# RWKV attention and a 16-expert layer on one core: two early experts split in two items, first steps reordered, one PSUM pool

## The chip, the cores and the metric

The kernel runs on one core of a Trainium2 chip. The metric is the device time of one execution in microseconds (us). The engines are called by the names of the profile: PE (TensorE matmul), PEld (its weight loads), DVE (VectorE), ACT (ScalarE), POOL (GpSimd) and SP (SyncE, which here only issues DMAs). PSUM is the memory that matmuls write[...].

## What is computed

An attention block with a decaying state, whose rows then go through a mixture of experts in two levels. Everything is f32. B, H, S, D are 4, 8, 768, 48; the 3072 rows have 384 columns; there are 4 groups of 4 experts, 1024 hidden columns each.

```python
for t in range(S):
    kt, vt, rt = (k[:, :, t], v[:, :, t], r[:, :, t])
    cur = np.einsum('bhd,bhe->bhde', u[None] * kt, vt)
    y[:, :, t] = np.einsum('bhd,bhde->bhe', rt, state + cur)
    state = w[None, :, :, None] * state + np.einsum('bhd,bhe->bhde', kt, vt)
...
x = attn_out.transpose(0, 2, 1, 3).reshape(B * S, H * D)
g_idx = np.argmax(x @ w_group, axis=1)
e_idx = np.argmax(xg @ w_expert[g], axis=1)
h = np.maximum(xg[mask_e] @ w1[g, e], 0.0)
ye = h @ w2[g, e]
out[tok_idx] = (g_w * e_w)[:, None] * ye
```

Each row goes to one expert only; `g_w` and `e_w` are the softmax weights of the chosen group and the chosen expert.

## The kernel before

**The token loop.** The 3072 rows are 24 tiles of 128 (`NT`). Step s of the loop at L714 handles tile s: 128 tokens of one batch entry, the four entries in turn, so four steps are one chunk of tokens, and a group of k, r and v loads (`load`, L284) holds two tiles. Inside a tile the recurrence is written as matmuls. k is scaled by powers of the inverse decay (`iw`) and r by powers of the decay (`pw`). `turn` (L435) transposes k or r of a tile on PE, and `turn_out` copies the result out of PSUM: k by ACT into `kT`, r by DVE, times `pw`, into `rT`. `scores` (L460) multiplies them into `PA`; `mask` (L478, DVE) copies the upper triangle into `am`, whose diagonal (the u term) was written before by `diagonal_here` (DVE) and `diagonal` (ACT, one instruction for each head). The diagonal comes from `own` (POOL: r times k times u, two products of 1.0 us) and `sum_own` (DVE). `values` (L509) multiplies `am` with v into the lower half of the two banks of `YB`; `state` (L497) adds what the earlier chunks left, and `update` and `carry` (L518, L529) renew that state R. `values_out` copies the result to `yT` on ACT. `scaled` (L425, POOL) makes the scaled k.

**Routing.** `rows_out` (L555) transposes `yT` back into rows, `gate_parts` and `gate_sum` make the 20 gate logits, and `route_1` to `route_5` choose the expert of each row, count places (`route_prefix`, on PE, with running sums `cum`), and scatter rows by indirect DMAs of POOL into `x_sorted` in device memory, one region of 3200 rows for each expert. After 12 tiles, in step 14, `choose_two` picks the two fullest experts; their weights are loaded in pieces (`early_piece`, 8 pieces of 384 KB for each expert) from step 16 on. After the last tile, `choose_rest` orders the other 14 by their counts, and `judge` decides whether a slow second pass is needed (L949); it is not run with these inputs.

**The expert stage** (L833 on) has 16 items, one for each expert, in the order of `SLOTS` (224 rows down to 164). For an item, `fetch_rows` loads rows, `columns` transposes them on DVE in blocks of 32 into `xe`, `up` runs 24 matmuls into `hT` (ReLU on ACT), `arrange` reorders w2 on ACT, `down` runs 24 matmuls whose result is still transposed, `finish` transposes it back on DVE, multiplies by the gate and scatters it in blocks of 32 rows by 4 quarters (6 or 7 indirect DMAs). Weights have two buffers: `fetch_weights(s + 2)` is issued behind the first `down` of item s.

**What sets the order.** The order on every engine is the order in which the code issues (`manual_schedule`, L76); semaphores come from the tiles' dependencies. SP, POOL, ACT, DVE and PE each work through their own queue in order. The loop has its own PSUM pool with six tiles (`PA`, `YB`: two banks each; `TR`, `RW`, `MS`, `SB`: one each); the expert stage opens another pool with four banks for `ph` and four for `po`. Ahead of the loop (L687 to L711) the first two tiles are prepared: `iw` is transposed into `RW`, k of tile 0 is scaled on DVE by it (`scaled_here`), and then turned.

Of the kernel before, what the change touches and what calls it, by code (L numbers as in the profile page):

```python
# [19 lines left out]
SLOTS = [224, 216, 212, 208, 208, 202, 202, 200, 200, 196, 194, 188, 186, 174, 172, 164]  # L20
# [7 lines left out]
def kernel(  # L28
# [78 lines left out]
    two_f = cst([P, 2], "two_f")  # L107
    two_i = cst([P, 2], "two_i", I32)
    cnt_s = cst([P, GE], "cnt_s")
# [112 lines left out]

    with ExitStack() as rec:
        ring = rec.enter_context(tc.tile_pool(name="ring", bufs=1))
        pool = rec.enter_context(tc.tile_pool(name="wkv", bufs=2))
        psum = rec.enter_context(tc.tile_pool(name="psum", bufs=1, space=bass.MemoryType.PSUM))

        def ps(shape, name):
            return psum.tile(shape, FP32, name=name)

        PA = ps([P, 2, 512], "PA")
        YB = ps([P, 2, 512], "YB")
        TR = ps([P, HC, P], "TR")
        RW = ps([P, NQ, P], "RW")
        MS = ps([P, 512], "MS")
        SB = ps([P, 512], "SB")
        y_ps = YB[:, :, 0 : 2 * P]
        RT = YB[:, :, 2 * P : 4 * P].rearrange("p b (h t) -> p b h t", t=P)
        lT_ps = TR[:, 0, :]
# [18 lines left out]
        SQ = spare([P, HC, 8])  # L258
        RK = spare([P, HC, 8])
        held_at = spare_at[0]  # L260
        SPARE = (held_at, held_at + 4 * NL, held_at + 4 * NL + 4 * GE)
# [36 lines left out]
        raw[0, "k"], raw[0, "r"] = place(0, "kt", 3), place(0, "rt", 3)  # L298
        for a in range(2):
            load_half(raw[0, "k"], k, 0, a, both[a])  # L300
            load_half(raw[0, "r"], r, 0, a, both[1 - a])
            if a == 0:
                nc.scalar.dma_start(
                    out=ub.rearrange("p h d -> p (h d)"),
                    in_=bass.AP(tensor=u.tensor, offset=u.offset, ap=[[0, P], [1, H * D]]),
                )
        zeros = ring.tile([P, XW], FP32, name="zeros")
# [4 lines left out]
        raw[0, "v"] = load(v, 0, "vt", 4)  # L312
        raw[1, "r"] = load(r, 1, "rt", 3)
        raw[1, "k"] = load(k, 1, "kt", 3)
# [3 lines left out]

        pw = ring.tile([P, HC, P], FP32, name="pw")
# [3 lines left out]
        make_identity(nc, ident)  # L323
        nc.gpsimd.memset(gwp, 0.0)
# [4 lines left out]
        for t in am[0:2]:  # L329
            nc.gpsimd.memset(t[:, 0], 0.0)  # L330
        nc.gpsimd.tensor_add(sel, ident[:, 0:NL], ident[:, 32 : 32 + NL])
        for q in range(2, NQ):
            nc.gpsimd.tensor_add(sel, sel, ident[:, 32 * q : 32 * q + NL])
# [499 lines left out]
    with ExitStack() as moe:  # L833
# [90 lines left out]
        for job in left:  # L924
            job()
# [294 lines left out]
```

## Time and profile before

| | us |
|---|---|
| median of 3 runs (lowest, highest) | 431.27 (428.61, 431.41) |
| the profiled execution, its own time | 432.07 |
| its span, first to last instruction | 430.3 |
| PE busy | 382.4 (89%) |
| POOL busy | 208.3 (48%) |
| ACT busy | 192.2 (45%) |
| DVE busy | 151.4 (35%) |
| moved by DMA | 82.02 MB, 191 GB/s |
| first `values` | 14.14 |
| last work of the loop on PE begins | 141.64 |
| first matmul of the expert stage | 159.77 |
| last copy out of PSUM begins | 417.75 |

The profile is that of one execution; all times in the text are counted from the start of its span. The clock of PE is the share of full speed that was granted (0.960 in the mean). Matmuls are pipelined and their ends are modelled, so what a series of them costs is read from start to start. An f32 matmul appears as two instructions, a transpose as one. A wait for several semaphores is put down to the one that came last.

### The profile page before, as it was taken

How to read it: one execution, taken by the hardware profiler on the slowest of the kernel's cores; microseconds unless marked ns; L12 is line 12 of the kernel's file. 1: busy time of each engine (PE TensorE's matmuls, PEld its weight loads, DVE VectorE, ACT ScalarE, POOL GpSimd, SP SyncE). 2: the span in 40 equal slices, each digit the busy share in tenths (PEclk: the TensorE clock that was granted, in tenths of full speed). 3: DMA queues.
4: the chain of work that ended last, by engine and by line, in shares of the span. 5: the costliest groups of instructions: out<-in, count | busy, mean ns of one | idle time of the engine just before them, and what ended most of it. 6: DMA issues, size and time to landing. Idle time of an engine off the chain costs nothing.

```text
span 430.3 us, 10330 instructions
## 1 busy us (share of the span) xinstructions
PE 382.4 (89%) x3874; PEld 366.1 (85%) x3874; DVE 151.4 (35%) x389; ACT 192.2 (45%) x461; POOL 208.3 (48%) x270
## 2 busy tenths in 40 slices
PE   2777999999798429999999999999999999999980
PEld 2556899988787319999999999999999999999970
DVE  6735788788666521102022022022022022022110
ACT  3668788887575122333424423423423424433410
POOL 7669939796812530062362452542542543352435
PEclk9999999999999858999999999999999999999995
DMA  9799989956969263979799889889899899999000
GB/s 146 111 168 172 205 179 205 201 112 149 218 187 272 105 175 54 248 175 268 169 236 270 184 224 263 206 238 246 216 245 243 219 248 261 220 269 247 23 23 27
DMA packets 122905, 82.02 MB, mean 191 GB/s; under 512 B 96420, under 2 KB 114020, under 8 KB 122848
## 3 DMA queue, kind: packets, MB, share of 16 engines
q1 hardware_dynamic: 114976, 70.98, 72.6%
q0 software_dynamic: 4960, 9.55, 7.8%
q10 hardware_dynamic: 2912, 0.77, 1.0%
q8 instruction: 32, 0.52, 0.6%
q14 instruction: 25, 0.20, 0.2%
HBM read 70.09 MB, written 11.68 MB: 190 GB/s over the span
## 4 chain that ended last, share of the span: by engine, by line
issue 44%; PE 24%; POOL 17%; DMA 6%; DVE 4%; ACT 3%; POOLq 1%; DVEq 0%; ACTq 0%
POOL out_dram L916 16%; PE PA L472 5%; PE YB L513 5%; DMA out_dram<-yt,idn 5%; PE TR L442 3%; ACT am L491 2%; PE YB L504 2%; PE YB L442 2%; PE RW L558 2%; PE TR L548 2%; PE MS L524 1%; DVE am L479 1%; PE MS L572 1%; POOL x_sorted L215 1%; DMA x_sorted<-xt,place_i 1%
## 5 line engine op out<-in xcount | busy, mean ns | idle before, releaser
L916 POOL DMA_INDIRECT out_dram<-yt,idn x107 | 104.0, 972 | 166.6 <-DVE yt L914 124.6
L892 PE MATMUL ph<-xe,w 128*128 128x200 f32 (+12 forms) x768 | 132.6, 333 | 7.9 <-DMA w<-in_moe_w_dram 7.9
L892 PEld LDWEIGHTS ph<-xe,w 128*128 128x128 f32 x768 | 129.8, 192 | 8.4 <-ACT w2p L882 8.0
L904 PE MATMUL po<-hT,w2p 128*128 128x200 f32 (+12 forms) x768 | 130.4, 330 | 0.0
L904 PEld LDWEIGHTS po<-hT,w2p 128*128 128x128 f32 x768 | 128.1, 190 | 0.0
L913 DVE STREAM_TRANSPOSE yt<-yT 128x672 f32<-128x672 f32 (+1 forms) x16 | 13.6, 847 | 209.8 <-ACT yT L907 209.8
L897 ACT ACTIVATE hT<-ph 128x416 f32<-128x416 f32 (+12 forms) x64 | 31.9, 498 | 101.1 <-PE ph L892 101.1
L491 ACT ACTIVATE am<-ident,du 128x128 f32<-128x128 f32 x184 | 60.5, 397 | 6.1 <-DVE du L431 6.0
L882 ACT COPY w2p<-w 128x1024 f32<-128x1024 f32 x48 | 47.0, 1046 | 11.9 <-POOL yT L839 11.9
L907 ACT COPY yT<-po 128x208 f32<-128x208 f32 (+12 forms) x48 | 15.5, 322 | 69.2 <-PE po L904 67.3
L215 POOL DMA_INDIRECT x_sorted<-xt,place_i x24 | 24.0, 998 | 36.5 <-ACT lT L553 27.4
L479 DVE COPY_PREDICATED am<-later,PA 128x1024 f32<-128x1024 int32 x24 | 31.5, 1313 | 6.7 <-PE PA L472 6.6
L513 PE MATMUL YB<-am,vt 128*48 128x128 f32 x384 | 27.0, 282 | 5.2 <-DVE am L479 2.6
L513 PEld LDWEIGHTS YB<-am,vt 128*48 128x48 f32 x384 | 20.5, 125 | 10.2 <-issue 4.9
L422 POOL TENSOR_TENSOR dg<-rp,kt 128x384 f32<-128x384 f32 x24 | 24.2, 1009 | 6.7 <-DMA rp<-in_r_dram 4.7
L472 PE MATMUL PA<-rT,kT 48*64 48x128 f32 (+1 forms) x736 | 25.8, 258 | 0.0
L423 POOL TENSOR_TENSOR dg<-dg,ub 128x384 f32<-128x384 f32 x24 | 24.2, 1007 | 2.0 <-DMA ub<-in_u_dram 0.2
L472 PEld LDWEIGHTS PA<-rT,kT 48*64 48x64 f32 x736 | 20.1, 134 | 4.3 <-issue 4.0
L426 POOL TENSOR_TENSOR kp<-kt,T 128x384 f32<-128x384 f32 x22 | 22.3, 1012 | 2.7 <-DMA kt<-in_k_dram 2.7
L542 ACT COPY yT<-YB 128x512 f32<-128x512 f32 x24 | 14.0, 582 | 17.2 <-PE YB L513 17.2
L455 DVE TENSOR_TENSOR rT<-YB,pw 128x512 f32<-128x512 f32 x22 | 15.2, 691 | 17.4 <-PE YB L442 14.6
L451 ACT COPY kT<-TR 128x512 f32<-128x512 f32 x24 | 14.0, 585 | 11.8 <-PE TR L442 11.8
(137 smaller groups left out, 313.9 us busy)
## 6 DMA issues: line engine op xcount, KB each, us to landing
w<-in_moe_w_dram SPq DMA_DIRECT2D x128, 384.0 KB, 9.4
vt<-in_v_dram SPq DMA_DIRECT2D x24, 192.0 KB, 5.1
kt<-in_k_dram SPq DMA_DIRECT2D x23, 192.0 KB, 4.2
rp<-in_r_dram SPq DMA_DIRECT2D x23, 192.0 KB, 5.8
xg<-x_sorted SPq DMA_DIRECT2D x42, 85.8 KB, 3.9
out_dram<-yt,idn POOLq DMA_INDIRECT x107
x_sorted<-zeros SPq DMA_DIRECT2D x4, 392.0 KB, 6.1
xg<-x_sorted SPq DMA_DIRECT2D x20, 73.5 KB, 5.3
```

What stands on the lines that cost most here:

```text
L215: ins = nc.gpsimd.indirect_dma_start(out=xs_dram, out_offset=bass.IndirectOffsetOnAxis(ap=place_i[:, i : i + 1], axis=0), in_=xt[:, i].rea ...
L422: nc.gpsimd.tensor_mul(dg, raw[g, "r"][:, a], raw[g, "k"][:, a])
L423: nc.gpsimd.tensor_mul(dg, dg, ub)
L472: nc.tensor.matmul(PA[64 * z : 64 * (z + 1), e, P * hc + 64 * z : P * (hc + 1)], lhsT=kT[rows, hc, 64 * z : 64 * (z + 1)], rhs=rT[rows, hc ...
L479: nc.vector.copy_predicated(am[n % NAM], later.unsqueeze(1).unsqueeze(1).to_broadcast([P, 2, HC, P]).bitcast(I32), PA.rearrange("p e (h t) ...
L491: nc.scalar.mul(am[n % NAM][:, e, hc, :], ident, du[:, e, hc : hc + 1])
L513: nc.tensor.matmul(y_at(e, hc), lhsT=vt[:, n % 2, 2 * hc + e, :], rhs=amn[:, e, hc, :], start=(n < 4 and hc < 2), stop=True, skip_group_ch ...
L882: nc.scalar.copy(o4[:, kk], v4[:, kk])
L892: nc.tensor.matmul(ph[:, i, 0:n], lhsT=w1[:, ko, P * (f + i) : P * (f + i + 1)], rhs=xe[:, ko].rearrange("p i b -> p (i b)")[:, 0:n], star ...
L897: nc.scalar.activation(hTs[s][:, f : f + 2, 0:n], ph[:, :, 0:n], AF.Relu)
L904: nc.tensor.matmul(po[:, 0:n], lhsT=w2p[:, d, fo, :], rhs=hT[:, fo, 0:n], start=(fo == 0), stop=(fo == FO - 1))
L916: ins = nc.gpsimd.indirect_dma_start(out=out_q, out_offset=bass.IndirectOffsetOnAxis(ap=idn[:, i : i + 1].bitcast(U32), axis=0), in_=yt[:, ...
```

## The change

1. *Two items for each early expert.* The first 128 rows (`AHEAD`) of each of the two early experts are loaded in step 21 (`rows_ahead`), transposed in step 23, and run through both projections right behind the loop (`up_ahead`, `down_ahead`), between the parts of the last routing. Their rest (96 and 88 rows) are items of the expert stage: one first, one last. The second projection of all four uses `hT` as the stationary operand and w2 as the moving one (`rows_down`), so its result has whole rows and goes out in one indirect DMA.
2. *The choice* is moved: the keys are made in step 14 and the choice in step 15; k, r and v that would be loaded in step 16 are issued ahead of it. A count over 16 tiles in step 22 (`bases`) tells how many rows of the two experts were taken ahead.
3. *The expert stage* has three weight buffers that rotate, besides that of the expert held for the last item; weights are fetched for item p + 3. `ph` takes four banks in turn and `po` two, out of one PSUM pool that serves the loop too.
4. *The first steps.* k and r of tile 0 are turned unscaled and multiplied by `iw` and `pw` on DVE; in steps 0 to 5 (`CLOSE`) the scores of the next tile and the rows of the last stand in front of the turns, and the gate logits of the first tiles are put off to steps 3 to 7. u comes as one row that a matmul spreads. Five of eight diagonals of a first tile are written by DVE, the others by ACT. Loads of groups 1 and 2 are issued ahead of the gate weights. Small constants are made in other steps.
5. *Banks.* The turned r goes to `RW`, the rows of `rows_out` to the upper half of `YB`, and the gates use `MS` and `TR` in turn at first.

The diff, cut to its core:

```diff
-SLOTS = [224, 216, 212, 208, 208, 202, 202, 200, 200, 196, 194, 188, 186, 174, 172, 164]
+AHEAD = 128
+SLOTS = [96, 88, 212, 208, 208, 202, 202, 200, 200, 196, 194, 188, 186, 174, 172, 164]
...
+    def rows_down(hT, w2, i, n, po, yt):
+        for fo in range(FO):
+            nc.tensor.matmul(
+                po[0:n, 0:DM], lhsT=hT[:, fo, 0:n], rhs=w2[:, fo, :], start=(fo == 0), stop=(fo == FO - 1),
+                skip_group_check=True,
+            )
+        nc.scalar.mul(yt[0:n], po[0:n, 0:DM], tagA[i][0:n, 1:2])
+        ins = nc.gpsimd.indirect_dma_start(
+            out=out, out_offset=bass.IndirectOffsetOnAxis(ap=idA[i][0:n].bitcast(U32), axis=0),
+            in_=yt[0:n], in_offset=None, bounds_check=N - 1, oob_is_err=False,
+        )
...
-        for hc in range(HC):
-            nc.tensor.transpose(RW[:, hc, :], iw[:, hc], ident)
-        turn(0, "rT", MS.rearrange("p (h t) -> p h t", t=P), early=True)
-        scaled_here(0, 0)
-        own(0, 0)
-        turn(0, "kT")
-        turn_out(0, "rT")
+        turn(0, "rT", MS.rearrange("p (h t) -> p h t", t=P))
+        turn_first()
+        for hc in range(HC):
+            nc.tensor.transpose(rows_ps[:, hc // 2, P * (hc % 2) : P * (hc % 2 + 1)], iw[:, hc], ident)
+        nc.scalar.copy(
+            T2.rearrange("p (b y) d -> p b y d", b=2),
+            rows_ps.rearrange("p b (y x) -> p b y x", x=DP)[:, :, :, 0:D],
+        )
+        own(0, 0)
+        scaled(0, 1)
+        own(0, 1)
+        scaled(0, 0)
...
+            if s == NT - 9:
+                loads(g + 1)
+            if s == NT - 3:
+                rows_ahead(0)
+                rows_ahead(1)
...
             values(s)
-            update(s)
             values_out(s)
+            if s == 0:
+                own_term(1)
+            for n, e, hc in waiting:
+                diagonal(n, e, hc, hc + 1)
+            if s <= CLOSE:
+                scores(s + 1)
+                update(s)
+                if s == CLOSE:
+                    sum_own(s + 3)
+                mask(s + 1)
             carry(s)
-            far = s + (3 if s > 2 else 2)
+            far = s + (2 if s < CLOSE else 3)
+            if 1 <= s < CLOSE:
+                rows_out(s - 1)
             if far < NT:
                 turn(far, "kT")
+                turn(far, "rT")
...
         c = NB - 1
+        out_0 = up_ahead(0, 0, PA[:, 0, 0:256])
         gate_sum(NT - 1)
         rows_out(NT - 1)
+        out_0()
         route_1(c)
         route_e(c)
         route_2(c)
-        route_p(c)
+        up_ahead(0, 2, YB[:, 0, 0:256])()
+        up_ahead(0, 4, TR.rearrange("p q t -> p (q t)"), partial(route_p, c))()
         route_3(c)
         route_4(c)
         route_5(c, range(4))
         choose_rest()
-        judge(same)
+        judge()
+        for i in range(2):
+            tokens(i, AHEAD, base_f[:, i : i + 1])
+        up_ahead(1, 0, PA[:, 0])()
+        down_ahead(0, YB[:, 0])
+        up_ahead(1, 4, RW.rearrange("p q t -> p (q t)"))()
+        down_ahead(1, TR.rearrange("p q t -> p (q t)"))
...
         fetch_rows(0)
-        for job in left:
-            job()
         fetch_rows(1)
-        arrange(0)
+        fetch_weights(1)
+        fetch_rows(2)
+        fetch_weights(2)
         columns(0)
...
+            if order[p] < 2:
+                rows_down(hTs[p], held(p)[1], 2 + i, SLOTS[i], po, yt)
+            else:
+                down(p, 0)
+            if p + 3 < last:
+                fetch_weights(p + 3)
```

`up_ahead(i, f, bank)` runs the matmuls of `up` for 128 columns, two or four column groups at a time, and gives back the ReLU as a call; `order` is experts 1 to 15 and then 0; `rows_ahead(i)` is four DMAs of rows and one of row numbers and gates.

## The prediction

> **What bounds the kernel now.** I read four views in this order: the page's 40 slices, the windows around the end of the token loop, the timeline of TensorE at the start, and the timeline of the last 14 us.
>
> The slices say that TensorE is the bound for most of the span, and where it is not:
>
> ```profile
> PE   2777999999798429999999999999999999999980
> ...
> PEclk9999999999999858999999999999999999999995
> DMA  9799989956969263979799889889899899999000
> ```
>
> One slice is 10.76 us. TensorE is short of work in slices 0 to 3, in slices 13 to 15 (8, 4, 2), and after the last full slice. From slice 16 on the expert matmuls run without a hole, so only these three places can give time back; a fourth is a cost, work added to the packed part.
>
> ```profile
> 142.40:159.70 17.30, 2.94 (x14) 2.23 (x14) 8.56 (x46) 3.86 (x7) 7.41 (x11) 0.63 0.41 125
> 159.70:171.00 11.30, 11.23 (x48) 10.86 (x49) 1.35 (x5) 1.63 (x3) 0.00 (x0) 0.80 0.46 99
> ```
>
> These are windows: length, then busy time of PE, PEld, DVE, ACT, POOL, then clock. For 17.3 us between loop and experts TensorE has 2.9 us of work, waiting for routing of the last chunk, for its scatter and for the rows to come back. The first up projection then runs at a mean clock of 0.80.
>
> ```profile
> 14.14 1.08 PE L513 MATMUL YB<-am,vt 128*48 128x128 f32 x16 [1.13 <-DVE am L479]
> ...
> 26.62 1.08 PE L513 MATMUL YB<-am,vt 128*48 128x128 f32 x16 [1.43 <-DVE am L479]
> ...
> 43.38 1.67 PE L513 MATMUL YB<-am,vt 128*48 128x128 f32 x16
> ...
> 58.81 1.08 PE L513 MATMUL YB<-am,vt 128*48 128x128 f32 x16
> ...
> 63.59 0.65 PE L513 MATMUL YB<-am,vt 128*48 128x128 f32 x8
> ```
>
> Each line is one step's `values` (steps 0, 2, 4, 7, 8). Step 7 to 8 takes 4.78 us, with TensorE packed; from 0 to 2 a step takes 6.2 us, from 2 to 4 it takes 8.4. The waits noted are for the mask (`am`), the last product of a chain that begins with the loads.
>
> ```profile
> 418.08 0.78 DVE L913 STREAM_TRANSPOSE yt<-yT 128x576 f32<-128x576 f32 x1 [11.78 <-ACT yT L907]
> 418.90 0.76 DVE L914 TENSOR_TENSOR yt<-yt,xg 128x576 f32<-128x576 f32 x1
> 419.93 0.97 POOL L916 DMA_INDIRECT out_dram<-yt,idn  x1 [6.00 <-DVEq L950]
> ...
> 426.31 0.97 POOL L916 DMA_INDIRECT out_dram<-yt,idn  x1 [0.30 <-issue]
> ```
>
> After the last matmul (417.7) come a copy (0.29), a transpose, a product and six scatters 1.28 us apart. The last ends at 427.28 and the span at 430.3, so a scatter takes 3.0 us to land.
>
> **Two prices used below.** Per moved column:
>
> ```profile
> 305.78 8.28 PE L904 MATMUL po<-hT,w2p 128*128 128x200 f32 x48
> 313.90 8.12 PE L892 MATMUL ph<-xe,w 128*128 128x196 f32 x48
> ```
>
> 24 f32 matmuls (48 instructions) of 200 columns take 313.90 - 305.78 = 8.12 us, 1.69 ns a column. Per weight load:
>
> ```profile
> 138.06 0.30 PEld L572 LDWEIGHTS MS<-sel,lT 128*128 128x128 f32 x2
> 138.28 0.30 PEld L176 LDWEIGHTS MS<-ohe,later 128*128 128x128 f32 x2
> 138.51 0.30 PEld L179 LDWEIGHTS MS<-cum,ones 128*128 128x128 f32 x2
> ```
>
> Pairs of loads of 128 columns start 0.22 to 0.23 us apart whether 20 or 64 columns are moved through them, so a load of 128 columns sets a pace of 0.112 us and a short matmul hides under it: 48 instructions take at least 5.4 us.
>
> **Behind the loop.** The change takes the first 128 rows of the two early experts out of the expert stage and runs them where TensorE stood still.
> - *One piece of 128 rows.* Up: 24 matmuls of 128 columns, 24 x 128 x 1.69 = 5.2, by the load pace 5.4 us. Down in row form: 8 matmuls of 384 columns, 8 x 384 x 1.69 = 5.2 us. Together 10.6, two pieces 21.2.
> - *One remainder (88 or 96 rows).* The up is not in the trace. Below: columns alone, 3.6 and 3.9 us; above: load plus columns unhidden, 48 x (112 + 77) ns = 9.1. I take the load pace, 5.4, because 20 and 64 columns gave one pace. Down 5.2. Together 10.6 each, 21.2 for both. The skill's TensorE: Matmul & The Clock Gate (Back-to-back issue gap) states about 81 ns for a load and matmul of 128 columns; that would make an up 3.9 us and save 6 us over four of them. The rows here are f32 at 112 ns, so the rows stand.
> - *Before, the same 440 rows* took from 159.77 to 197.66 (the first matmul of 212 columns): 37.9 us, of which 2.3 is clock[...]. The same page (The HAM clock gate) has half rate until one busy window of 3.4 us has passed, which would be 1.7 us. With the row the gain from closing the hole is 0.6 larger; I count whole stretches and so the row.
> - *TensorE after the loop.* It is free at 142.07 in the old time. 21.2 us of pieces, 1.4 of gate sum, row transposes, prefix and count (pitches 0.22, 0.5, 0.45, 0.22) and about 0.5 of waiting for the one-hots: 165.2. The gate sum stands behind two column groups of the first up, 1.3 us, so routing starts 0.9 later; the prefix stands behind another, and the count behind three more, so the choice comes 2 us later (150.0 to about 152). This lies beside 15.8 us of early work (the second up and both downs), so costs nothing. Next item: 165.2 + 10.6 = 175.8; the 14 whole experts 417.7 - 197.7 = 220.0 more, 395.8; the last remainder 406.4. Against 417.7: **-11.3**.
> - *Cover of the first loaded weights.* SP waits for the scatter (landed 154.6, about 2 later after), then issues nine row loads and tag loads (2.23 us per four, so 5) and eight weight pieces: from about 163, landing 8.7 us later (w1, measured on issue to landing), 172. They are needed at 175.8. Nothing, with 4 us spare; without that cover the price is the lateness itself. Later items have three buffers and an item takes about 12 us of transfers in 16 of matmuls (in the windows between 307 and 319 us), so they stay covered.
> - *End.* The last item is a remainder in row form: one scaled copy (0.48, as the 128x384 `xt` copy L562), 0.1 and 0.27 of handover, one scatter 0.97, landing 3.0: 4.8 instead of 12.6. **-7.8**.
>
> **First steps.** What is removed from the chain ahead of `values(0)`: r and k are turned unscaled and multiplied on DVE (0.69 each), so k no longer waits for iw's transpose and the scaling (0.55). DVE's chain ends at 7.6 as before; then 0.7 + 0.7 + reduce 0.54 + five diagonals (0.75 x 5/4 = 0.9) + mask 1.3 = 11.8. Before 14.14. Next limits: POOL makes one tile in 3.0 us (three products of 1.0), which gives `values` of 1, 2, 3 at about 15.5, 19, 22. Then loads bind. Ahead of the loop SP now issues v0, k1, r1, k2, v1, r2 before the gate weights: six pairs at 3 us, then 3 us of gates, done at 24 rather than 26.3 for the same loads; k3, v2, r3 follow at 2 us each and v2 lands 5.1 us after, near 31. `values(4)` at 31 instead of 43.4. From there 4 steps of 4.8 plus the put-off gate work (about four pairs of 0.6) and one extra turn and scores (1.8): step 8 at 53.5 instead of 63.6. **-10**. Both ends: -5 if half is given back to loads that land as late as now (POOL gets r of the third group at 25.5); -13 if POOL's 3.0 and TensorE's 4.8 a step alone set it.
>
> Small moved work: u comes as one row, spread by one matmul and one copy (0.48, as L562) before POOL's first product at 6.3; ACT zeroes two masks of 640 columns (0.4 per 256 columns at L361, so 1 us each) where it waited 4.2 us for TR; POOL's constants move one to three steps later (0.2 to 0.5 each, with the gate copy some 3 us over steps 2 to 7), where it has 1.8 us spare in each 4.8. Without that cover they would delay a tile by as much: inside the -5.
>
> **The steady loop** has the same instructions. Exchanged banks (turned r to RW, rows to YB's upper half) swap one copy (0.69 DVE) for another (0.48 ACT) ahead of `state`; it lies ahead of `state` by 0.3 us or more: 0, from -3 to +3. The loads taken in front of the choice remove SP's wait for it (10.6 us) from k, v and r; the PE stall at 112.9 to 115.1 is marked "issue", not a load, so I count nothing for it. Rows ahead: ten more DMAs on SP (5 us of its queue, by 2.23 per four) that wait for the scatter of chunk 3 in step 20; behind them stand seven weight pieces, needed only after the loop. Two DVE transposes (about 0.5 each) follow in the last step, where DVE is idle. All fit if rows land by step 23. The sums for the bases, eight of 0.2 on DVE, lie there too.
>
> **Sum.** 430.3 - 11.3 - 7.8 - 10 = 401.2 span. The profiled run took 432.07, 1.77 beyond its span and 0.8 above the median: 401.2 + 1.8 - 0.8 = 402.2.
>
> **The rivals.**
> - *The start gives half (0.2).* Loads set the first steps: DMA share is 1.39 and 1.14 in 20:40 us at 184 and 174 GB/s. For it: POOL's 4.7 us wait for r at 25.5. Against: SP issued gate weights in between. -5 rather than -10: 407.
> - *First weights or rows late (0.15).* A 9 us slip in SP makes TensorE wait 5 us and cool, 2.3 more: 409.5; with half a start 414.
> - *Slower: DVE blocked by the rows ahead (0.07).* The two transposes stand on DVE ahead of the last routing; rows wait on SP for a scatter on POOL, with weight pieces between. Before, pieces waited 9.4 us for POOL. Each us that rows land after step 23 begins is one us of everything. It outweighs the 29 us gained, and 4 more for a visible loss, at 33 us of lateness; a single POOL wait of 9.4 and a loading time of 10 give 417. It needs a circle of such waits: then 436 or more.
> - *Nothing (0.04).* The pieces run, but the expert stage becomes bound by transfers: weights 3.15 MB, rows and results 0.65, 14 times, 53 MB in 220 + 29 us, so below 213 GB/s. For it: the stage moves 217 to 254 GB/s now. Against: single us in 300:303 show 348 to 376, others 28. That the early split does not fit, and the second pass runs, I leave out: by the reference's inputs the chosen experts have 137 and 138 rows in 16 tiles, and 128 are split off.
>
> The likeliest, with 0.54, is 402. The range 394 to 415 takes in the larger start (-3), prices of the remainders (-3.5 to +7), half a start and late weights. A difference of 1% is about what this measurement tells from none: the first three cases are faster, 0.89; same 0.04; slower 0.07.
>
> **What would show it.** `values(4)` near 31 and step 8 near 54; TensorE busy from loop to experts with no wait above 1 us, clock near 1.0; the first matmul of 212 columns about 34 us after the loop's last; remainders' ups of 5.4 us; one scatter at the end. Wrong if transposes of the rows ahead wait for DMA, if TensorE waits on `w` after the pieces, or if the first steps show waits for `rp` or `kt`.

## The result, and the profile after

| | before | after |
|---|---|---|
| median, us (lowest to highest) | 431.24 (428.61 to 431.41, 4 runs) | 403.01 (401.20 to 405.57, 4 runs) |
| ratio, 95% interval | | 0.936 (0.930 to 0.943) |
| the profiled execution, its own time | 432.07 | 403.92 |
| its span | 430.3 | 402.1 |
| PE busy | 382.4 (89%) | 390.3 (97%) |
| granted clock, mean | 0.960 | 0.992 |

The kernel became 28 us faster; 402 was forecast. Executions over 1.5% above the fastest of their kernel are called slow: ratios in this document use the others alone, and the profiles of experiments 3, 4, 6 and 8 are of slow ones.

The slices of the page of the changed kernel, one digit for 10.05 us:

```profile
PE   8999999999999999999799999999999999999993
...
PEclk9999999999999999999899999999999999999998
DMA  9989999995966949999999999999989999861000
```

Of the three places where TensorE was short of work, the start and the hole behind the loop have filled up. The last slice holds less than a slice of work. One new digit stands out: a 7 in slice 19, with an 8 in the clock. That is a wait which the prediction did not have.

The `values` of steps 0, 1, 2, 4 and 8 on the timeline of TensorE, changed kernel:

```profile
12.17 1.08 PE L579 MATMUL YB<-am,vt 128*48 128x128 f32 x16
16.20 1.08 PE L579 MATMUL YB<-am,vt 128*48 128x128 f32 x16 [0.26 <-DVE am L539]
20.30 1.08 PE L579 MATMUL YB<-am,vt 128*48 128x128 f32 x16
...
29.81 1.08 PE L579 MATMUL YB<-am,vt 128*48 128x128 f32 x16
...
54.24 1.08 PE L579 MATMUL YB<-am,vt 128*48 128x128 f32 x16
```

The waits for the mask, 1.1 to 1.4 us before, are 0.26 once. The windows behind the loop (length, then busy time of PE, PEld, DVE, ACT and POOL with the number of instructions, then clock, DMA share and GB/s), up to the first whole expert, and over the 14 whole experts:

```profile
127.60:150.20 22.60, 22.57 (x143) 18.22 (x141) 8.68 (x52) 4.09 (x11) 8.75 (x9) 1.00 0.78 224
150.20:160.70 10.50, 10.50 (x65) 7.88 (x64) 1.22 (x4) 1.85 (x5) 2.40 (x3) 1.00 1.03 258
160.70:384.90 224.20, 221.81 (x1346) 221.40 (x1345) 37.68 (x83) 79.18 (x140) 85.57 (x88) 0.99 0.91 224
```

In the first two TensorE is busy for all but 0.03 us at full clock. In the third it lacks 2.4 us. The end, on the timeline:

```profile
395.56 0.58 ACT L242 ACTIVATE yd<-YB,tagA 96x384 f32<-96x384 f32 x1 [4.83 <-PE YB L238]
396.42 0.94 POOL L243 DMA_INDIRECT out_dram<-yd,idA  x1 [1.76 <-ACT yd L242]
```

One copy and one scatter, where six scatters stood. The scatter's instruction ends at 397.36; the span ends 4.7 us later.

Read as stretches on TensorE, predicted and measured (the before column is the profile of before). "Loop's last" is `values` of step 23.

| stretch | before | predicted | after |
|---|---|---|---|
| start to step 8 | 63.6 | 53.5 | 54.2 |
| step 8 to loop's last | 76.2 | 76.2 | 71.2 |
| loop's last to first 212 columns | 57.8 | 36.0 | 35.3 |
| 14 whole experts | 220.0 | 220.0 | 224.2 |
| last remainder | in the above 57.8 | 10.6 | 10.6 |
| behind the last matmul | 12.6 | 4.8 | 6.6 |
| span | 430.3 | 401.1 | 402.1 |

(36.0 is 2.25 from step 23 to the free TensorE of the old profile, and 33.7. The 57.8 holds all the rows of both early experts.) Three stretches are within 0.7 us. Three are off, by -5.0, +4.2 and +1.8, and those nearly cancel. The experiments are about them and about the reasons for the rest.

### The profile page after: what moved, and what is told of

It reads as the page before. It is cut to its first block, busy times and chain, and to the rows that moved or that the text cites. A ratio compares the mean times of both kernels' runs of the same rounds, so it can differ in the third digit from the quotient of the medians.

```text
span 402.1 us, 10465 instructions
## 1 busy us (share of the span) xinstructions
PE 390.3 (97%) x3963; PEld 363.4 (90%) x3963; DVE 153.4 (38%) x406; ACT 179.7 (45%) x429; POOL 201.1 (50%) x265
## 4 chain that ended last, share of the span: by engine, by line
issue 48%; PE 25%; POOL 20%; DVE 3%; DMA 1%; POOLq 1%; ACT 1%; ACTq 0%
POOL out_dram L1119 16%; PE YB L579 5%; PE PA L532 4%; PE TR L507 2%; PE YB L570 2%; PE RW L507 2%; PE MS L590 1%; PE YB L626 1%; DMA x_sorted<-xt,place_i 1%; DVE am L539 1%; PE TR L615 1%; POOL x_sorted L228 1%; PE RW L418 1%; PE MS L640 1%; POOL dg L485 1%
## 5 line engine op out<-in xcount | busy, mean ns | idle before, releaser
L1107 PE MATMUL YB<-hT,w2p 128*128 128x208 f32 (+10 forms) x336 | 58.7, 328 | 0.0
L1107 PE MATMUL PA<-hT,w2p 128*128 128x208 f32 (+10 forms) x336 | 58.1, 326 | 0.0
L1107 PEld LDWEIGHTS YB<-hT,w2p 128*128 128x128 f32 x336 | 55.8, 190 | 0.0
L1107 PEld LDWEIGHTS PA<-hT,w2p 128*128 128x128 f32 x336 | 55.3, 190 | 0.0
L1067 DVE STREAM_TRANSPOSE xe<-xg 128x672 f32<-128x672 f32 (+2 forms) x16 | 12.7, 797 | 96.3 <-DMA xg<-x_sorted 89.0
L1095 PE MATMUL SB<-xe,w 128*128 128x208 f32 (+12 forms) x192 | 34.5, 332 | 2.4 <-DVE xe L1067 2.4
L1095 PEld LDWEIGHTS SB<-xe,w 128*128 128x128 f32 x192 | 32.4, 198 | 3.4 <-DVE xe L1067 2.7
L1095 PE MATMUL TR<-xe,w 128*128 128x208 f32 (+12 forms) x192 | 32.8, 321 | 0.0
L1095 PE MATMUL MS<-xe,w 128*128 128x208 f32 (+12 forms) x192 | 32.8, 321 | 0.0
L1095 PE MATMUL RW<-xe,w 128*128 128x208 f32 (+12 forms) x192 | 32.8, 321 | 0.0
L1095 PEld LDWEIGHTS MS<-xe,w 128*128 128x128 f32 x192 | 30.7, 191 | 0.0
```

Source lines behind the costliest of these rows:

```text
L1067: nc.vector.transpose(xe[:, :, 0:nb, :], xg[:, 0:nb, 0:QW].rearrange("p i (ko a) -> p ko i a", a=32))
L1095: nc.tensor.matmul(ph[:, i, 0:n], lhsT=w1[:, ko, P * (f + i) : P * (f + i + 1)], rhs=xe[:, ko].rearrange("p i b -> p (i b)")[:, 0:n], star ...
L1107: nc.tensor.matmul(po[:, 0:n], lhsT=w2p[:, d, fo, :], rhs=hT[:, fo, 0:n], start=(fo == 0), stop=(fo == FO - 1))
```

## The experiments

The kernels of one series ran on one chip, the three series on different ones. Series 1 has the kernel before beside it, but not the changed kernel. The kernel before took 431.2 beside the result, 437.9 beside 1 to 4, 437.1 beside 5 to 8 and 429.4 beside 9 to 12. So times are compared inside a series, or by their ratio to the kernel before.

### Series 1: the wait for rows, and the loop

**1. Rows of the fourth item in front of the third item's weights.**

```diff
         fetch_rows(1)
         fetch_weights(1)
+        columns(0)
         fetch_rows(2)
+        fetch_rows(3)
         fetch_weights(2)
-        columns(0)
...
-            if 0 < p and p + 2 < GE:
+            if 1 < p and p + 2 < GE:
```

> The changed kernel, with the rows of the fourth item of the expert stage issued ahead of the weights of the third (nothing else moves). Theory: in the changed kernel TensorE waits before the fourth item, 2.5 us for its rows plus 1.8 us of half clock, because these rows stand on SP behind two experts' weights. Then this kernel has no wait there, the 14 whole experts take 220 us instead of 224.2, and the time is about 4 us shorter, near 399. Rival: the rows are late because the transfers as a whole are late; then the wait only moves to the weights of the third item (first matmul of 208 columns) and the time stays at 402 to 404.

417.48 us (414.83 to 423.61), ratio 0.950 (0.945 to 0.956). The fourth item has no wait. The fifth has it instead, as the timeline of TensorE shows:

```profile
225.52 4.41 PE L1095 MATMUL SB<-xe,w 128*128 128x202 f32 x12 [3.14 <-DVE xe L1067]
```

The fifth item's rows stand in SP's queue where the fourth's had stood. The wait belongs to the place in the queue, not to the item. The gain that was expected did not come: with the wait of 3.1 us, half clock behind it (4.41 us for 12 instructions, 2.21 later) and a wait of 1.9 marked "issue" at 381.7, the 14 whole experts took 229.5 us, not 220.

**2. Two weight buffers in turn instead of three, the early expert's among them.**

```diff
-            for i in range(2)
+            for i in range(1)
...
-            return early[0] if p == last else turns[p % 3]
+            return early[0] if p == last else turns[p % 2]
...
-        fetch_weights(2)
...
-            if p + 3 < last:
-                fetch_weights(p + 3)
+            if p + 2 < last:
+                fetch_weights(p + 2)
```

> The changed kernel with two rotating weight buffers instead of three (weights fetched two items ahead, as before the change). Theory of the prediction: three buffers give the cover after the choice; with two, the third item's weights can start only when the first item is done with its own (about 155 to 161 us), land near 172, and are needed at 178, so it is only just covered: no change within 2 us at that place. Theory of the late rows: the second prefetched expert is what the rows stand behind, so with two buffers the 2.5 us wait before the fourth item is gone as well and the time is about 4 us shorter. Rival: the weights of the third item come late and TensorE waits 3 us or more there.

414.95 us (412.89 to 418.93), ratio 0.944 (0.939 to 0.950). No item waits for rows; two waits of 0.55 and 0.93 us are for the copy of a result (`yT`). With one expert's weights fewer in front of them the rows come in time: an item's rows now stand in front of its own weights, and DVE has transposed the fourth item's at 197.18, 11.3 us before TensorE takes them up at 208.51. The ratio lies between those of the changed kernel (0.932 to 0.966), so no sign is left that the gain rests on the third buffer.

**3. Loads of step 16 behind the choice, as before the change.**

```diff
-            if s % 2 == 0 and g < NG and s != NT - 8:
+            if s % 2 == 0 and g < NG:
                 loads(g)
-            if s == NT - 9:
-                loads(g + 1)
```

> The changed kernel with k, r and v of step 16 issued behind the wait for the choice again, as before the change. The steps from 8 to 23 took 76.2 us before and 71.2 after; the difference is two stalls marked issue and a slower clock behind them. If the loads in front of the choice removed these stalls, they come back here: steps 8 to 23 take 75 to 76 us, the time is 4 to 5 us longer. If the stalls are of another kind (instructions that arrive late while the first weights are loaded), nothing comes back: 71 to 72 us.

427.47 us, with four runs between 413.6 and 430.2: too wide for a ratio. SP waited 15.9 us for the choice again. From step 19 to 20 TensorE took 13.5 us. But experiment 2, in the same series and with the loads in front, shows 13.3 us there. So the order of the loads isn't separated from the stall by this run. The fourth item waited for its rows here too, 3.7 us.

**4. The kernel before, with the loads in front of the choice.**

```diff
-            if s % 2 == 0 and g < NG:
+            for x in [g] if s % 2 == 0 and s != NT - 8 else [g + 1] if s == NT - 9 else []:
...
```

> The kernel before with one edit: k, r and v of step 16 are issued in step 15, in front of the wait for the choice. If these loads carry the 5 us by which the middle of the loop got shorter, steps 8 to 23 take 71 to 72 us instead of 76.2 and the time falls to about 426. If not, they stay at 75 to 77 and the time at 429 to 431.

436.86 us (432.73 to 440.18), ratio 0.997 (0.993 to 1.001): no difference. Step 8 to 23 took 77.0 us, against 76.2 in the profile of before, with a step of 7.7 in it. This part of the change brings nothing on its own, and the 5 us of the middle are not its doing.

### Series 2: is it the change, the chip, or the place

**5. The changed kernel again.** No edit.

> The changed kernel itself, so that the others of this series have it beside them on one chip. Both theories of the middle of the loop speak of its steps 16 to 20. Theory A (the gain of 5 us there belongs to the change, since loads stand in front of the choice): steps 8 to 23 take 71 us again, no step over 6 us. Theory B (the stall comes and goes with the chip and the run, and the first profile of the changed kernel happened to have none): one or two of steps 16 to 20 last 7 us or more, marked as issue, and the time is 5 to 12 us longer than in the first profile on that account. The rest should repeat: first steps done at 54, one wait of 2 to 3 us for rows at the fourth item, 6.6 us behind the last matmul.

421.33 us (418.76 to 424.43), ratio 0.966 (0.957 to 0.974). The same instructions, 17.4 us longer in span. Start to step 8 is 54.25 again and the end 6.4. The middle takes 80.5 (+9.4), loop's last to 212 columns 38.6 (+3.3), the whole experts 229.1 (+4.9). Behind the loop, TensorE waits 1.7 us for ACT's late copy of the last result, and half clock follows; among the experts it waits 4.5 us for ReLU results on ACT and 1.7 marked "issue". The middle shows it best. Three groups of the timeline of TensorE in the first profile of the changed kernel (`state`, `values`, `update`):

```profile
108.53 0.66 PE L570 MATMUL YB<-rT,R 48*48 48x128 f32 x14
109.12 1.08 PE L579 MATMUL YB<-am,vt 128*48 128x128 f32 x16
110.03 0.53 PE L590 MATMUL MS<-vt,kp 128*48 128x48 f32 x16
```

and the same instructions in this run:

```profile
109.68 0.27 PE L570 MATMUL YB<-rT,R 48*48 48x128 f32 x1
110.29 0.33 PE L570 MATMUL YB<-rT,R 48*48 48x128 f32 x2 [0.34 <-issue]
...
111.77 0.47 PE L570 MATMUL YB<-rT,R 48*48 48x128 f32 x3 [0.40 <-issue]
112.51 1.39 PE L570 MATMUL YB<-rT,R 48*48 48x128 f32 x8 [0.28 <-issue]
113.83 0.66 PE L579 MATMUL YB<-am,vt 128*48 128x128 f32 x3
...
116.11 1.11 PE L579 MATMUL YB<-am,vt 128*48 128x128 f32 x8 [0.56 <-issue]
```

Fourteen `state` matmuls took 0.6 us there; here two or three come every 0.7 us. Nothing that the profile knows holds them ("issue"), so no wait for data shows. Then the clock falls, in the windows of this run:

```profile
110.00:115.00 5.00, 3.37 (x22) 1.56 (x23) 0.00 (x0) 0.53 (x2) 3.72 (x4) 0.70 1.03 281
115.00:120.00 5.00, 4.44 (x40) 3.93 (x37) 2.54 (x5) 1.58 (x4) 0.64 (x8) 0.50 0.41 144
```

22 matmuls in 5 us, and the next 5 at half clock. Theory B of the expectation holds: the stall is not a trait of either kernel. It may be one of the chip: all eight profiles of series 1 and 2 have it (the middle takes 76.2 to 81.9 us), and of the four of series 3 one, for 1.5 us.

**6. The second expert's piece left out.** Both projections of its first 128 rows are not computed.

```diff
-        up_ahead(1, 0, PA[:, 0])()
...
-        up_ahead(1, 4, RW.rearrange("p q t -> p (q t)"))()
-        down_ahead(1, TR.rearrange("p q t -> p (q t)"))
```

> Leaves out both projections of the second expert's first 128 rows, so those rows are missing from the output; their loads and everything else stay. Theory 'TensorE sums' (my prediction's): the piece costs its 10.6 us and the whole is 10.6 us shorter, against the changed kernel on the same chip. Theory 'cover': the piece lies over a wait for rows and weights of the next items that would be there anyway: the scatter's rows come back at 147.8 and the first loaded weights land at 160 to 162, so TensorE stands still some 8 us instead, cools, and the whole is 0 to 3 us shorter. The cover theory wants a new wait on w or xe behind the pieces of 6 us or more and a clock of half for some us after it.

425.79 us (415.38 to 430.31); the spread is too wide for a ratio. TensorE behind the first piece's `down`:

```profile
142.72 5.41 PE L238 MATMUL YB<-w,hTA 128*128 128x384 f32 x16
153.69 2.83 PE L1092 MATMUL SB<-xe,w 128*128 128x88 f32 x12 [5.56 <-DVE okA L256]
```

It waits 5.6 us for the rows of the first remainder (DVE's transpose of them waited for their DMA until 153.00), then runs that remainder's up at half clock (2.83 us for 12 instructions, 1.47 in the changed kernel). The remainder takes 17.4 us instead of 10.5. So from the loop's last to the first 212 columns it is 40.1 us, against 38.6 with the piece, though 10.6 us of work are gone. The wait is what the cover theory wants. The time is less clear: this profile is of an execution of 424.5 us with half clock for 14 us of work, and the shortest of the four took 415.4, which is 5.9 below experiment 5's median. So of the piece's 10.6 us the wait covers at least half; whether it covers all is not shown.

**7. A whole expert last.** Both remainders first, four weight buffers in turn.

```diff
-        order = list(range(1, GE)) + [0]
+        order = [1, 0] + list(range(2, GE))
...
-        turns = [early[1]] + [
+        turns = [early[1], early[0]] + [
...
-            return early[0] if p == last else turns[p % 3]
+            return turns[p % 4]
...
-        fetch_weights(1)
         fetch_rows(2)
         fetch_weights(2)
+        fetch_weights(3)
...
-            if p + 3 < last:
-                fetch_weights(p + 3)
+            if p + 4 < GE:
+                fetch_weights(p + 4)
```

> Both remainders run first, then the 14 whole experts with four buffers of weights in turn, so the last item is a whole expert with its copy, transpose, product and six scatters behind it. Theory of the sum: the end costs 12.6 us as before the change, not 6.6, so +6; and the fourth item's rows have 10.6 us more of TensorE work ahead of them, so its wait and cold matmul (4.2) are gone or smaller: +2 in all. Rival (a last scatter of 96 whole rows and one of 128 pieces of rows cost the same, and what counts is how many bytes are still on their way): the end is within 2 us of the changed kernel's and the whole 2 to 4 us shorter.

434.0 us (431.31 to 438.88), ratio 0.989 (0.981 to 0.997), 12.7 us longer than experiment 5. The end is as the sum had it:

```profile
420.92 0.30 ACT L1110 COPY yT<-YB 128x164 f32<-128x164 f32 x1 [2.19 <-PEq L1161]
...
429.48 0.97 POOL L1119 DMA_INDIRECT out_dram<-yt,idn  x1 [0.30 <-issue]
```

From the last copy to the span's end (433.1) it is 12.2 us, where experiment 5 has 6.3: 5.9 us more. The other half of the expectation failed: the wait for rows didn't shrink, it grew. Timeline of SP (DMA issues), of DVE and of TensorE:

```profile
177.40 5.83 SPq L133 DMA_DIRECT2D w<-in_moe_w_dram  x4
185.12 6.40 SPq L139 DMA_DIRECT2D w<-in_moe_w_dram  x4
192.87 5.75 SPq L1049 DMA_DIRECT2D xg<-x_sorted  x4
```

```profile
207.31 0.88 DVE L1067 STREAM_TRANSPOSE xe<-xg 128x672 f32<-128x672 f32 x1 [39.47 <-DMA xg<-x_sorted]
```

```profile
208.24 4.47 PE L1095 MATMUL SB<-xe,w 128*128 128x208 f32 x12 [8.79 <-DVE xe L1067]
```

A fourth buffer let one more expert's weights into SP's queue in front of the rows. They are issued at 193, and TensorE loses 8.8 us and then 2.2 to a cold clock (4.47 instead of 2.27).

**8. Early weights issued later.**

```diff
-            some = 1 if s == NT - 8 else 2 if s < NT - 1 else 3
+            some = {19: 2, 20: 3, 21: 3, 22: 4, 23: 4}.get(s, 0)
```

> The sixteen pieces of early weights are issued in steps 19 to 23 (2, 3, 3, 4, 4) instead of from step 15 on. If TensorE's stall in steps 16 to 20 comes with the burst of these transfers (its instructions arrive late behind them), it is gone from steps 15 to 19 and may come back in steps 20 to 23; if it comes from the choice itself, from the place in the program or from the chip's own state, it stays at 105 to 123 us. Price: the second expert's weights land some 5 to 8 us later, about 140 instead of 132, needed at 139: 0 to 3 us of waiting behind the loop. If the stall is on this chip 8 us long and goes, the whole is 5 to 8 us shorter than the changed kernel; if not, 0 to 3 longer.

418.79 us (413.01 to 421.40), ratio 0.951 (0.941 to 0.961), an interval that overlaps experiment 5's. SP runs ahead of TensorE and issued the first pieces at 104, not 94.7. The stall stayed: step 19 to 20 took 8.4 us, with "issue" marks at 110.2, 113.6 and 115.6, and the fourth item waited 2.2 us for its rows. Five pieces had been issued by then, so this doesn't clear the transfers either.

### Series 3: a cure for the rows, and what is left

**9. The changed kernel a third time.** No edit.

> The changed kernel a third time, beside the next ones. If the stall of the token loop is the chip's or the run's own, its length differs again from 0 us (first profile) and from about 9 us (second profile); the first steps (step 8 at 54.2), the pieces (the ups 5.3, the downs 5.2) and the end (6.3 to 6.6 us behind the last matmul) repeat within 0.3 us. The ratio to the kernel before lies between the two seen so far, 0.936 and 0.966.

400.60 us (399.43 to 401.26), ratio 0.932 (0.928 to 0.937). Start to step 8 54.5, middle 72.4, to the 212 columns 35.3, whole experts 220.0, last remainder 10.6, end 6.5. Two "issue" marks in the middle come to 0.87 us. The fourth item didn't wait.

**10. Rows fetched three items ahead, in front of the same item's weights.**

```diff
         fetch_weights(2)
+        fetch_rows(3)
         columns(0)
...
-            if 0 < p and p + 2 < GE:
-                fetch_rows(p + 2)
+            if 0 < p and p + 3 < GE:
+                fetch_rows(p + 3)
...
-            xg = xgs[p] = pool.tile([P, 8, QX], FP32, tag="xg", bufs=3, name="xg")
+            xg = xgs[p] = pool.tile([P, 8, QX], FP32, tag="xg", bufs=4, name="xg")
```

> Rows are fetched one item earlier, in front of the weights of the same item instead of behind them, with four buffers of rows instead of three; nothing else differs. Theory 'rows wait in SP's queue behind the weights of later items': no expert item waits for xe any more, also not the fourth and the fifth, and nothing else takes its place, since the weights are delayed by one fetch of rows only (0.3 MB, about 1.2 us at 250 GB/s): 2 to 4 us shorter than the changed kernel where that one has its wait of 2.4 us and a cold matmul, 0 to 1 where it has none. Rival 'transfers bind the stage': the wait comes back as one for weights (ReLU or the result's copy late behind the rearranging of w2), and the time is the same within 1 us.

400.21 us (399.35 to 403.28), ratio 0.934 (0.929 to 0.939): the same as experiment 9, which had no wait to remove. The waits of DVE show what changed (in total, times, longest), first of experiment 9, then of this one:

```profile
DVE xe L1067 <- DMA xg<-x_sorted: 133.5, 13, 15.8
```

```profile
DVE xe L1067 <- DMA xg<-x_sorted: 23.3, 3, 15.1
```

DVE waits for rows three times instead of thirteen, and no expert item waits on TensorE; the whole experts take 219.8 us. The changed kernel puts an item's rows behind its own weights, not behind those of later items; here, as in experiment 2, they stand in front of them. The fourth item shows what that is worth. DVE's transpose of its rows and TensorE's first matmul on them, in experiment 9:

```profile
195.31 0.88 DVE L1067 STREAM_TRANSPOSE xe<-xg 128x672 f32<-128x672 f32 x1 [10.45 <-DMA xg<-x_sorted]
196.24 2.38 PE L1095 MATMUL SB<-xe,w 128*128 128x208 f32 x12
```

and in this one:

```profile
182.55 0.87 DVE L1067 STREAM_TRANSPOSE xe<-xg 128x672 f32<-128x672 f32 x1
194.70 2.27 PE L1095 MATMUL SB<-xe,w 128*128 128x208 f32 x12
```

In experiment 9 the rows were ready 0.05 us before they were needed, here 11.3 us. So experiment 9 only just escaped the wait, and this placing removes its cause, though by time it beats nothing that was seen.

**11. All early weights behind the loop.**

```diff
-            some = 1 if s == NT - 8 else 2 if s < NT - 1 else 3
-            for job in left[0:some]:
-                job()
-            del left[0:some]
...
-        assert not left
+        for job in left:
+            job()
```

> All sixteen pieces of early weights are issued behind the loop's last step, so no weights move while steps 15 to 22 run. Theory 'TensorE's stall in the loop comes with the transfer of weights': steps 15 to 23 take 4.4 to 5.5 us each, no row is marked issue between 100 and 125 us, and step 23 starts at 125 to 127. Rival 'it belongs to that place of the program': the stall of 5 to 9 us at 105 to 120 stays. The price behind the loop is known: sixteen pieces of 384 KB at 300 to 390 GB/s are 16 to 20 us, of which TensorE waits 8 to 14; the whole is so much longer less the stall.

419.13 us (one run). Not one "issue" mark between 100 and 125; the middle takes 70.9 us. But experiments 10 and 12, with the weights in the loop and on the same chip, take 70.9 as well. So it doesn't decide what makes the stall. It does give the price of the cover that early loading provides, on TensorE:

```profile
139.81 2.90 PE L786 MATMUL PA<-xeA,w 128*128 128x128 f32 x12 [12.53 <-DMA w<-in_moe_w_dram]
...
152.81 4.42 PE L786 MATMUL PA<-xeA,w 128*128 128x128 f32 x24 [3.40 <-DMA w<-in_moe_w_dram]
```

15.9 us of waiting, and the time is 18.5 longer.

**12. Gate weights in front of the loads of groups 1 and 2.**

```diff
-        raw[1, "k"] = load(k, 1, "kt", 3)
-        raw[1, "r"] = load(r, 1, "rt", 3)
-        raw[2, "k"] = load(k, 2, "kt", 3)
-        raw[1, "v"] = load(v, 1, "vt", 4)
-        raw[2, "r"] = load(r, 2, "rt", 3)
...
         gates_in()
+        raw[1, "k"] = load(k, 1, "kt", 3)
...
```

> The loads of groups 1 and 2 are issued behind the gate weights again; the rest of the first steps is as changed. My prediction's step: the gate weights are 3 us of SP's queue that stood in front of the second and third group, so step 4 starts some 3 us later, at 32.5 to 33 instead of 29.8, and step 8 at 57 instead of 54.2. Rival (TensorE and POOL set the first steps, the loads are covered): steps 4 to 8 within 0.7 us of the changed kernel's.

400.64 us (one run). The `values` of steps 4 and 8 of this kernel, then of experiment 9:

```profile
29.64 1.08 PE L579 MATMUL YB<-am,vt 128*48 128x128 f32 x16
...
54.09 1.08 PE L579 MATMUL YB<-am,vt 128*48 128x128 f32 x16
```

```profile
30.01 1.08 PE L579 MATMUL YB<-am,vt 128*48 128x128 f32 x16
...
54.47 1.08 PE L579 MATMUL YB<-am,vt 128*48 128x128 f32 x16
```

Not later, but 0.4 us earlier, and that much it was earlier at step 0 already (12.04 against 12.41). The rival holds: these loads, which SP issued 1.6 to 5 us later than in experiment 9, are covered. From k of group 3 and v of group 2 on, SP's queue had caught up (19.3 and 21.4, against 20.5 and 21.6), so later loads are not tested by this.

## Why the prediction was right, and where it was not

**Behind the loop: right, and for its reason.** The pieces were to cost nothing but their length, since TensorE stood still there. The stretch came out 0.7 us below the sum, with the ups of the remainders at 5.3 (predicted 5.4) and the downs at 5.2. Taking the load pace of 0.112 us for the remainders, and not the columns alone, was the right end of the bound. Experiment 6 shows the other side: without one piece TensorE waits 5.6 us, so that at least half of the piece lies in time that is lost anyway. The cover of the first loaded weights held too: no wait at 160.7.

**The end: right in kind, 1.8 us too small.** Predicted 4.8, measured 6.6; experiment 7, which undoes it, gives 5.9 us back. The mis-sized term is the landing, "one scatter 0.97, landing 3.0": the span ends 4.7 us behind the instruction. Nor are the 3.0 us all landing. In the trace of before, SP's wait for the last scatter ends 1.2 us behind the instruction (428.46), and 1.9 us more pass while the engines close the program. In the changed kernel these are 2.2 (399.58) and 2.5. So 1.0 of the 1.7 us is the landing: I took its price from the last of six scatters that carry 128 quarter rows each, and one scatter of 96 whole rows is another transfer. It repeats: 2.1 in experiment 5, and 1.2 in experiment 7, which has the six scatters again. Whether the size or the form of the scatter makes it was not tried. The other 0.6 is the closing, where POOL's last drain ends 1.1 us behind SP's, 0.3 in before.

**First steps: the time right, the bound wrong.** Step 8 was predicted at 53.5 and came at 54.2. (The terms from 31 on, four steps of 4.8, 2.4 and 1.8, add up to 54.4, not 53.5.) But POOL's 3.0 us a tile and "then loads bind" name the wrong limits. Steps 0 to 4 are 4.0 to 5.5 us apart, so steps 1 to 3 came 0.7 to 2.4 us later than forecast, and step 4, at 29.8 instead of 31, earlier. v of group 2, whose landing was to set step 4, landed at 27.7, 2.1 us before its use; and experiment 12 issues the loads of groups 1 and 2 later, and nothing moves. TensorE's own work sets these steps: it is busy for 19.2 of the 20 us from 20 to 40. Of the gain of 9.4 us, 2.0 is the shorter chain to step 0 (14.14 to 12.17). Most of the rest is waiting of TensorE that is gone: 8.1 us between 14 and 44 in before, for masks, for copies on ACT, and 1.8 marked "issue", against 1.3 between 12 and 54 after. Which part of the change removes which wait is argued from the order alone; they were not undone one by one.

**The whole experts: a step missing, up to 4.2 us.** "Later items have three buffers ... so they stay covered" looked at weights alone. What came late was the small load. SP's queue in the first profile of the changed kernel, rows (`xg`) and weights, and what DVE and TensorE did:

```profile
160.50 4.62 SPq L133 DMA_DIRECT2D w<-in_moe_w_dram  x4
165.31 2.10 SPq L139 DMA_DIRECT2D w<-in_moe_w_dram  x4
168.76 5.75 SPq L133 DMA_DIRECT2D w<-in_moe_w_dram  x4
175.44 6.03 SPq L139 DMA_DIRECT2D w<-in_moe_w_dram  x4
182.56 5.84 SPq L1049 DMA_DIRECT2D xg<-x_sorted  x4
```

```profile
196.41 0.88 DVE L1067 STREAM_TRANSPOSE xe<-xg 128x672 f32<-128x672 f32 x1 [10.00 <-DMA xg<-x_sorted]
```

```profile
191.98 2.98 PE L1107 MATMUL PA<-hT,w2p 128*128 128x208 f32 x16
197.34 4.04 PE L1095 MATMUL SB<-xe,w 128*128 128x208 f32 x12 [2.39 <-DVE xe L1067]
201.22 2.27 PE L1095 MATMUL MS<-xe,w 128*128 128x208 f32 x12
```

Sixteen weight pieces, those of the third item and of the fourth itself, stand in front of the fourth item's rows, and rows take 9.5 us to land (median). TensorE loses 2.4 us, and then 1.8 to the clock (4.04 against 2.27). Shown by four moves: the wait goes one item on when one fetch is moved (1), grows to 8.8 with a fourth buffer (7), and the rows come 11.3 us ahead of their use with one buffer fewer (2) or when fetched earlier (10). It is small enough to be there in some runs and not in others: 2.4 us in the first profile, 3.7 in experiment 3, 2.2 in 8, 0.7 in 12, none in 5 and 9. Where it was absent in series 3, the 14 experts took 220.0 (9), which is the sum's number.

**The middle of the loop: predicted 0, measured -5.0, and 0 is nearer to what the change does.** The step that failed is "it is marked issue, not a load, so I count nothing for it": I left the stall of before in the sum as if it belonged to the loop. The stall also stands in the prediction's line of slices, as the 7 of slice 10 (107.6 to 118.4 us), which its list of places short of work passes over; the 8, 4, 2 that it gives as slices 13 to 15 are slices 12 to 14. The timeline of before at that place:

```profile
112.38 0.54 PE L504 MATMUL YB<-rT,R 48*48 48x128 f32 x7
115.08 0.43 PE L504 MATMUL YB<-rT,R 48*48 48x128 f32 x7 [2.15 <-issue]
115.44 1.15 PE L513 MATMUL YB<-am,vt 128*48 128x128 f32 x16
116.36 0.86 PE L524 MATMUL MS<-vt,kp 128*48 128x48 f32 x16
```

With the half-clock stretch behind it the two steps took 7.25 and 6.85 us, where the same steps of the changed kernel took 4.79 and 5.27: 4.0 too many. Another 1.17 "issue" stands at 136.7. Without these, before has 71.0 us in the middle. The changed kernel has 70.9 in experiments 10 to 12 and 71.2 in its first profile; with its own stall it had 72.4 (9) and 80.5 (5). So the clean loops are equal within 0.3 us, as the sum had it. The first pair of profiles differs by 5 us there because before had the stall and after had none; in series 2, where the changed kernel has a longer one, only 15.8 of the 28 us are left (0.966).

What makes the stall stays open. "Issue" marks of 0.4 to 1.9 us also stand among the whole experts in most profiles of series 1 and 2, so it isn't bound to the loop, and the chip, which changed with the series, is not separated from the rest. For transfers: in all runs that have it, early weights are moving, and in experiment 11, where none are, TensorE's instruction packets come evenly. These are the 16 KB packets of the queue called instruction, which I take to be TensorE's, since one comes for about 6 us of its work. Their starts, from the trace:

```
experiment 11    85.2   90.1   96.9  102.9  108.8  115.1  121.3
before           89.1   94.4  100.2  112.3  118.4  123.6
experiment 5     85.3   90.7  101.3  106.3  110.8  124.7
```

In before TensorE stood from 112.9 to 115.1, and the packet that was due at 106 started at 112.3. Late instructions behind weights would fit that. In experiment 5 the trickle goes on for 5 us after the packet of 110.8, which a late packet alone doesn't explain. And experiments 10 and 12 have weights moving and no stall. So the cause is argued, not shown.

**The rivals.** "The start gives half" didn't happen. "First weights or rows late" happened in small: not at the first weights but at the rows of the fourth item, at 4.2 us instead of 7. "DVE blocked by the rows ahead" didn't happen: TensorE goes from loop to pieces without a wait in the first profile. (In series 1 and 2 the changed kernels wait 1.7 to 2.5 us there, marked as ACT's copy of the last result or as "issue", not as DVE.) "Nothing", bound by transfers, didn't happen in the first profile; in series 2 the whole experts took 229.1 us, with waits of 4.5 us of the second projection for ReLU results.

The total was as near as 1 us because -5.0 stood against +4.2, +1.8 and small terms. The mechanisms behind 19 of the 29 us forecast, behind the loop and at the end, held; the 10 of the first steps came, but not by the limits named; and the closeness is partly luck.

## What to carry to other kernels

- Work moved into a hole costs its length only if it fits and its data are there; check that by taking it out again, as here, where 10.6 us less work brought a wait of 5.6 us.
- When buffers are added for a large load, look at the small loads in the same queue behind it. A fetch that is needed first must be issued first: ask of each queue not only whether it is fast enough but in which order it delivers.
- A stall marked "issue" in one profile isn't part of the kernel until a second profile shows it. Compare clean steps with clean steps, and take a sum's closeness apart by stretches before believing it.

## What the runs showed of the hardware

- TensorE can get two to four instructions each 0.7 us for some 7 us, with no wait on data (experiment 5), and the clock then falls to 0.50. Against the clean 70.9 us of the middle, the same kernel lost 0.3 (first profile), 1.5 (9) and 9.7 us (5).
- One scatter of 96 rows of 384 f32 had landed 2.2 us behind its instruction's end, the last of six of 128 quarter rows 1.2 us. From there to the span's end it took 2.5 and 1.9 us more.
- Four row loads of 86 KB hold SP for 1.9 us with no weights in front of them (146.3) and for 5.6 to 5.8 us behind weights (154.0, 182.6), in the first profile of the changed kernel. So transfers waiting in the queue also hold up the engine that issues.
